# Memory projections in column tiles of 160 over all heads, with the next operand by a masked sum and a VectorE block transpose

## The chip, the cores and the metric

The kernel runs on one NeuronCore of a Trainium2 chip. Its engines work side by side, each on its own list of instructions: PE (TensorE, matmuls; PEld is its weight loading), DVE (VectorE), ACT (ScalarE), POOL (GpSimd) and SP (SyncE, which here only issues transfers). The metric is the device time of one execution in microseconds. A profile is one further execution, with every instruction's start and duration.

## The reference

The program is the forward and the backward pass of a layer: a recurrent memory transformer A, gated by a SwiGLU block B. What the change touches is A, for one batch of S = 2048 tokens of width D = 640, 32 heads of 128, a memory of M = 8 rows and segments of 32 tokens:

```python
mem = mem0
outs = []
for s in range(n_seg):                       # 64 segments
    xs = x[:, s * seg_len:(s + 1) * seg_len, :].copy()
    h = jnp.concatenate([mem, xs], axis=1)   # 8 + 32 rows
    q = jnp.einsum('btd,dhe->bhte', h, Wq)
    k = jnp.einsum('btd,dhe->bhte', h, Wk)
    v = jnp.einsum('btd,dhe->bhte', h, Wv)
    scores = jnp.einsum('bhqe,bhke->bhqk', q, k) * scale
    scores = jnp.where(mask[None, None], scores, -1000000000.0)
    p = _softmax(scores, axis=-1)
    o = jnp.einsum('bhqk,bhke->bhqe', p, v)
    o = jnp.einsum('bhte,hed->btd', o, Wo)
    mem = o[:, :M, :].copy()
    outs.append(o[:, M:, :])
```

The result is `x + s * g`, with `s` from A and `g` the gate from B; the gradients of all inputs and weights are outputs too. The eight memory rows of a segment come out of the segment before it, so the 64 segments form a chain, forward and, for the gradients, backward.

## The kernel before

Six phases follow each other: layer norm; B forward, which also transposes B's weights; A forward (`phase3_Afwd`); the output rows that are still missing (`phase3b_out`); A backward (`phase4_Abwd`); the weight gradients of A (`phase6_Awgrads`); and B backward with the rest. In `phase3_Afwd` and `phase4_Abwd` the instructions of each engine are kept in the order in which they are written (`in_order`). Each of these phases is a loop over the 64 segments. A step of the loop is `chain(t, gap)`: the work on the memory rows, each part of which needs the one before it, with calls of `gap(...)` between the parts. In the gaps stand pieces of work that are free of the chain: the attention of the ordinary tokens in tiles of three segments. Such a tile has eight units of four heads, spread over three steps as 3, 3 and 2 units. WARM names short matmuls whose results nobody reads.

**A forward step.** `hx` holds the operand: 640 rows of D as 5 chunks of 128 partitions, and 32 columns, 8 of them memory rows of this segment and 24 later tokens that ride along. `packed_half` (L346) multiplies it with Wk, Wq and Wv. Four column tiles of PE work side by side, each on 32 output partitions and 512 columns. The memory attention follows (L539 to L580), and its result stands in `oTm`, 128 partitions by 32 heads by 32 columns. `packed_out` (L362) projects it with Wo. The heads are split in two halves and the 640 columns in two halves of 320, so four column tiles hold 2 x 2 partial results in the PSUM bank `pm`, after 16 rounds of four matmuls. `fold_add` (L375) adds the two halves of the heads: ACT copies 160 columns of the upper 64 partitions (L381), DVE adds them to the lower 64 (L382), twice, with one buffer `fup` used in turn. `fold_turn` (L392) turns the sum of 64 x 320 into the layout of `hx` by six small matmuls with a selection matrix (L398), and DVE copies the 8 memory columns into the next `hx` (L594). The sum itself goes to DRAM as FS (L595). The 24 riding columns are loaded from the transposed tokens XNT four steps at a time (`ride_ld`, L464) and copied into `hx` by POOL (`ride`, L487).

The fillers around this place: gap G4 has the softmax of the third unit (`soft`, L650), whose exponentials run on ACT, and the normalisations (`norm`, L666): a reciprocal on DVE (L671), a multiplication on POOL (L672) and a POOL transfer (L673) for each unit. Gap G5, between `fold_add` and `fold_turn`, has the transposes of the first unit's probabilities (`turn_p`, L680) and of queries (`turn_q`, L629), one WARM matmul and the transposes of one weight block (L295). Gap G6, after `fold_turn`, has `turn_p` of the second unit, `turn_q`, and the transposes of keys (`kprep`, L612) in two steps of three.

**A backward step** runs the same way with `gox` in place of `hx`. It starts with the projection by Wo transposed (L1076), and ends with three calls of `packed_out` with 8 columns each, by Wv, Wk and Wq transposed (L1117, L1138, L1140), which add up in one bank. Then come `fold_add`, gap G5 with units of `dprob` and `gmem` and two WARM matmuls, `fold_turn`, the copy into the next `gox` (L1145), two transfers of the sum to GWO (`fold_store`, L386), and gap G6 with DVE work (`dsoft`) and one WARM matmul. In `gap_of`, `ride_ld` and the loads for later steps stand on SP's queue.

**Around the loops.** The transposed weights are made in the gaps of the forward loop (`wT_A_units`, L286; the copies are L90 and L92). After the forward loop FS is copied into HRO and SR by POOL transfers, one for each backward step (`later`, L960 to L977).

Of the kernel before, what the change touches and what calls it, by code (L numbers as in the profile page):

```python
# [9 lines left out]
BF16 = mybir.dt.bfloat16  # L10
# [30 lines left out]
class K:  # L41
# [55 lines left out]
    def setup_consts(self):  # L97
# [16 lines left out]
        self.sel = sel  # L114
        with tc.tile_pool(name="mkscr", bufs=1) as scr:
            self.build_masks(const, scr)
# [35 lines left out]
    def setup_dram(self):  # L152
# [23 lines left out]
        self.FS = mk("FS", (T, 64, 320))  # L176
# [109 lines left out]
def wT_A_units(k, Wq, Wk_, Wv, Wo):  # L286
# [5 lines left out]
    def unit_qkv(nat, dstT, jc):  # L292
        def turn(pt):
            for dc in range(DC):
                nc.tensor.transpose(pt[:, dc, :], nat[:, dc, jc * P:(jc + 1) * P], k.ident[:])  # L295

        def store(st, pt, eng, q):
            k.copy(st[:], pt[:], eng=eng)
            q.dma_start(dstT[jc * P:(jc + 1) * P, :].rearrange("p (dc q) -> p dc q", q=P), st[:])
        return turn, store  # L300
# [61 lines left out]
def packed_out(k, pm, x, W, first, last):  # L362

    nq = x.shape[2]
    for i in range(16):
        for a in range(2):
            for b in range(2):
                h = 16 * a + i
                p0 = 32 * (2 * a + b)
                k.nc.tensor.matmul(pm[p0:p0 + nq, 0:320], x[:, h, :], W[:, h, 320 * b:320 * b + 320],  # L370
                                   start=(first and i == 0), stop=(last and i == 15),
                                   tile_position=(0, p0), skip_group_check=True)


def fold_add(k, pm, pool):  # L375

    nc = k.nc
    fs = pool.tile([64, 320], BF16, name="fsum", tag="fsum")
    for c in (0, 160):
        up = pool.tile([64, 160], F32, name="fup", tag="fup")  # L380
        nc.scalar.copy(up[:], pm[64:128, c:c + 160])  # L381
        nc.vector.tensor_tensor(fs[:, c:c + 160], pm[0:64, c:c + 160], up[:], ALU.add)  # L382
    return fs


def fold_store(eng, dst, fs):  # L386

    for b in range(2):
        eng.dma_start(dst[:, 320 * b:320 * b + 320], fs[32 * b:32 * b + 8, :])


def fold_turn(k, bank, fs):  # L392

    pt = bview(bank, P, k.DC, 8)
    for (dc, p0, c0, w, b) in ((0, 0, 0, 128, 0), (3, 0, 64, 128, 1), (2, 64, 0, 64, 1), (1, 0, 128, 128, 0),
                               (4, 0, 192, 128, 1), (2, 0, 256, 64, 0)):
        kw = {} if w == 128 else dict(tile_position=(0, p0))
        k.nc.tensor.matmul(pt[p0:p0 + w, dc, :], fs[:, c0:c0 + w], k.sel[0:64, b, :], start=True, stop=True,  # L398
                           skip_group_check=True, **kw)
    return pt  # L400


def phase3_Afwd(k, W4, Wv, Wk_):
# [6 lines left out]
    with tc.tile_pool(name="b0", bufs=1) as io, tc.tile_pool(name="b0s", bufs=3) as stp, \  # L410
# [3 lines left out]
        nc.sync.dma_start(xs[:], k.XNT[:, 0:k.NB0].rearrange("(dc p) t -> p dc t", p=P))  # L414
        wq = k.A_Wq.rearrange("(dc p) h e -> p dc (h e)", p=P)
        wo = k.A_Wo.rearrange("h e d -> e h d")
        fetch = [(Wq[:, dc], wq[:, dc]) for dc in range(DC)] + [(Wo[:, h:h + 8], wo[:, h:h + 8]) for h in range(0, H, 8)]
# [23 lines left out]
    with tc.tile_pool(name="ast", bufs=1) as st, tc.tile_pool(name="achain", bufs=1) as ch, \  # L441
# [11 lines left out]
        for i, tt in enumerate(kTs + hxs + qTs + xPs + PTs + [oTm, vt]):  # L453
# [3 lines left out]
        with nc.allow_non_contiguous_dma(reason="tiny mem0 transpose load"):  # L457
            for dc in range(DC):
                nc.sync.dma_start(hxs[0][:, dc, 0:8], k.mem0[:, dc * P:(dc + 1) * P].rearrange("m p -> p m"))
            nc.sync.dma_start(k.m_rows(k.HRO, 0), k.mem0)  # L460
# [3 lines left out]
        def ride_ld(t):  # L464
            x0 = k.NB0 + 24 * t
            b, sub = t // 4, t % 4
            if sub == 0 and x0 < S:
                w = min(96, S - x0)
                rt = ch.tile([P, DC, 96], BF16, name="ride", tag="ride")
                nc.sync.dma_start(rt[:, :, 0:w], k.XNT[:, x0:x0 + w].rearrange("(dc p) s -> p dc s", p=P))  # L470
                rides[b] = (rt, w)

# [13 lines left out]

        def ride(t):  # L487
            b, sub = t // 4, t % 4
            if k.NB0 + 96 * b >= S:
                return  # L490
            rt, w = rides[b]
            nc.gpsimd.tensor_copy(hxs[t % 2][:, :, 8:8 + w // 4], rt[:, :, sub:w:4])

        def chain(t, gap):
# [47 lines left out]
            sTm = ch.tile([40, 2, P], BF16, name="sTm", tag="fsum")  # L542
            nc.scalar.copy(sTm[:], psT.rearrange("p a q h -> p a (q h)"))
            if t + 1 < T:
                ride(t + 1)
# [23 lines left out]
            PTm = ch.tile([104, 8, 16], BF16, name="PTm", tag="fsum")  # L569
# [20 lines left out]
            fs = fold_add(k, pm, ch)  # L590
            gap("G5")
            pt = fold_turn(k, bC, fs)
            nxt = hxs[(t + 1) % 2]
            nc.vector.tensor_copy(nxt[:, :, 0:8], pt[:])  # L594
            nc.gpsimd.dma_start(k.FS[t], fs[:])  # L595
# [119 lines left out]
        ride(0)  # L715
# [110 lines left out]
def gx_ld(k, xs, x0, eng):  # L826
    w = min(P, k.S - x0)
    eng.dma_start(xs[:, :, 0:w], k.GST[:, x0:x0 + w].rearrange("(dc p) t -> p dc t", p=P))
# [13 lines left out]
def phase3b_out(k, Wo, W0, W4):  # L842
# [6 lines left out]
    src = k.WOT.rearrange("(dc p) j -> p dc j", p=P)  # L849
    fetch = [(WoT[:, dc], src[:, dc]) for dc in range(DC)]  # L850
# [112 lines left out]
    for s in range(3):  # L963
# [3 lines left out]
        for b in range(2):  # L967
# [3 lines left out]
            cols = slice(320 * b, 320 * b + 320)  # L971
            later.append((dst[:, :, cols], k.FS[t0:t0 + 3 * (n - 1):3, 32 * b:32 * b + 8, :]))
            t1 = t0 + 3 * (n - 1)
            later.append((k.HRO[r1:r1 + 8, cols], k.FS[t1, 32 * b:32 * b + 8, :]))
    for b in range(2):
# [1030 lines left out]
```

## Time and profile before

| what | value |
|---|---|
| runs of the kernel | 5575.35, 5579.72, 5584.14 us (median 5579.72) |
| the profiled execution | span 5565.9 us, mean granted PE clock 0.956 |
| busy in the span | PE 4988.2 us (90%), PEld 3177.3, DVE 2372.9, ACT 1836.6, POOL 1567.2 |
| forward loop with its start (533 to 1880 us) | 1347 us, PE busy 1216 |
| backward loop with its start (2175 to 3420 us) | 1245 us, PE busy 1152 |
| `packed_out` forward, L370 | 4032 matmuls of 320 columns, 63 calls |
| `packed_out` backward, L370 | 12288 matmuls of 320 columns, 192 calls |
| PE's matmuls waiting in the turn, L398 | 28.3 us forward, 24.2 us backward |

In the lines of the timeline the first number is the start in us from the span's start and the second the time from the first start to the last end in a run of equal instructions (xN of them). `out<-in` are the tiles, and in brackets stands how long the engine had been idle before it and what ended that. A matmul's duration contains its latency, and matmuls overlap, so N matmuls take less than N durations.

### The profile page before, as it was taken

The numbers are of one execution on the slowest core, as the hardware profiler recorded it, in microseconds if no ns is written. First come the engines' busy times: TensorE is split into PE (matmuls) and PEld (weight loads), VectorE is DVE, ScalarE is ACT, GpSimd is POOL, SyncE is SP. The second block draws the span as 40 slices with busy tenths as digits, with TensorE's granted clock in tenths as the row PEclk, the third lists the DMA queues.
The fourth block names the chain that finished last, engine by engine and source line by source line (L and its number), as shares of the span: only waits on it lengthen the run. The fifth ranks groups of instructions, "written<-read, shape, count | busy, mean of one in ns | idle before, by whom it ended". The sixth has DMA issues, their size and how long they took to land. (4 is left out here: it accounts for less than half of the span.)

```text
span 5565.9 us, 167384 instructions
## 1 busy us (share of the span) xinstructions
PE 4988.2 (90%) x67526; PEld 3177.3 (57%) x67870; DVE 2372.9 (43%) x7485; ACT 1836.6 (33%) x5040; POOL 1567.2 (28%) x2606
## 2 busy tenths in 40 slices
PE   4988989999999786999999997999999999999999
PEld 2544555555555453656666664666566656657565
DVE  5743555555555423444454542233233323311451
ACT  2432465555555522333333331232123222301111
POOL 0000244444444313333333333243223322310000
PEclk9999999999999787999999998999999999999999
DMA  7563456556555465666666665343334333546332
GB/s 252 185 206 95 139 170 174 168 167 175 162 164 154 125 202 170 182 189 187 184 185 186 181 171 126 89 121 97 83 93 121 93 85 95 141 161 214 104 119 92
DMA packets 1007174, 835.88 MB, mean 150 GB/s; under 512 B 505131, under 2 KB 894919, under 8 KB 1003083
## 3 DMA queue, kind: packets, MB, share of 16 engines
q1 hardware_dynamic: 760275, 570.63, 36.2%
q0 software_dynamic: 92560, 149.71, 9.5%
q10 hardware_dynamic: 153564, 104.81, 6.5%
q8 instruction: 535, 8.77, 0.7%
q14 instruction: 240, 1.97, 0.1%
HBM read 511.81 MB, written 324.39 MB: 150 GB/s over the span
## 5 line engine op out<-in xcount | busy, mean ns | idle before, releaser
L1460 PE MATMUL wg<-gr,hr 120*128 120x512 bf16 (+1 forms) x2640 | 591.0, 385 | 16.9 <-DVE dST L1392 12.9
L1438 PE MATMUL g<-w,gT 128*128 128x320 bf16 x3840 | 548.9, 300 | 0.0
L1460 PEld LDWEIGHTS <-hr 120*128 120x128 bf16 (+1 forms) x2640 | 258.6, 99 | 341.3 <-issue 49.0
L1438 PEld LDWEIGHTS <-gT 128*128 128x128 bf16 x3840 | 368.9, 98 | 136.6
L251 POOL DMA_DIRECT2D r<-GOS x256 | 143.0, 563 | 798.3 <-PE r6p L1402 749.3
L90 DVE CAST wgo<-wg 128x512 bf16<-128x512 f32 x72 | 47.5, 688 | 586.1 <-issue 280.1
L351 PEld LDWEIGHTS <-hx 128*32 128x32 bf16 x7680 | 178.3, 96 | 167.9 <-issue 8.4
L90 DVE CAST stg<-bank 128x512 bf16<-128x512 f32 x256 | 177.1, 692 | 206.7 <-PE bank L351 194.1
L370 PEld LDWEIGHTS <-gkv 128*8 128x8 bf16 x8192 | 190.9, 88 | 104.3 <-DVE gkv L1069 24.6
L661 ACT ACTIVATE xP<-xsp,xnm 120x120 bf16<-120x120 f32 (+1 forms) x704 | 239.9, 374 | 8.6 <-DVE xnm L657 5.4
L92 ACT CAST wgo<-wg 128x512 bf16<-128x512 f32 x48 | 25.8, 589 | 638.2 <-PE wg L1460 638.2
L1447 DVE TENSOR_TENSOR ghacc<-ghacc,g 128x320 f32<-128x320 f32 x240 | 117.2, 488 | 277.9 <-PE g L1438 277.9
L1405 ACT CAST gr<-r6p 120x512 bf16<-120x512 f32 (+1 forms) x176 | 103.1, 586 | 362.3 <-PE r6p L1402 340.0
L1220 POOL DMA_DIRECT2D DSR<-gdS x176 | 101.7, 578 | 424.4 <-DVE gdS L1218 391.1
L710 POOL DMA_DIRECT2D OR<-xv x163 | 93.8, 576 | 425.2 <-ACT xv L709 295.5
L92 ACT COPY gT<-t6g 128x960 bf16<-128x960 bf16 (+5 forms) x216 | 166.8, 792 | 120.0 <-PE t6g L1421 119.5
L672 POOL TENSOR_TENSOR xP<-xP,xrz 120x480 bf16<-120x480 bf16 x163 | 161.7, 992 | 149.7 <-DVE xrz L671 99.7
L1218 DVE SCALAR_TENSOR_TENSOR gdS<-gdp,Dx,gPr 120x120 bf16<-120x120 f32 (+1 forms) x680 | 182.9, 331 | 0.0
L1421 PE MATMUL t6g<-ident,gr 120*128 120x120 bf16 (+1 forms) x2112 | 171.1, 220 | 3.6 <-DVE wgo L90 3.1
L370 PE MATMUL bank<-Wo,oTm 128*32 128x320 bf16 x4032 | 173.9, 333 | 0.0
L1289 PE MATMUL gbank<-WqT,ident 128*128 128x512 bf16 x453 | 156.4, 394 | 19.5 <-issue 11.7
L536 DVE COPY vt<-stg 8x512 bf16<-8x512 bf16 x512 | 163.0, 318 | 24.3 <-ACT stg L92 17.2
(360 smaller groups left out, 11183.6 us busy)
## 6 DMA issues: line engine op xcount, KB each, us to landing
QVS<-stg SPq DMA_DIRECT2D x128, 256.0 KB
gqv<-QVS SPq DMA_DIRECT2D x108, 192.0 KB
vTt<-VTD SPq DMA_DIRECT2D x64, 320.0 KB
VTD<-gvT POOLq DMA_DIRECT2D x168, 120.0 KB, 3.4
OR<-xv POOLq DMA_DIRECT2D x163, 120.0 KB, 2.7
DSR<-gdS POOLq DMA_DIRECT2D x168, 112.5 KB, 3.5
dS<-DSR SPq DMA_DIRECT2D x168, 112.5 KB
P<-PR SPq DMA_DIRECT2D x168, 112.5 KB
```

What stands on the lines that cost most here:

```text
L90: return nc.vector.tensor_copy(out, in_)
L92: return nc.scalar.copy(out, in_)
L351: k.nc.tensor.matmul(bank[32 * g:32 * g + 32, :], x[:, dc, :], W[:, dc, c0:c0 + 512], start=(dc == 0), stop=(dc == k.DC - 1), tile_positio ...
L370: k.nc.tensor.matmul(pm[p0:p0 + nq, 0:320], x[:, h, :], W[:, h, 320 * b:320 * b + 320], start=(first and i == 0), stop=(last and i == 15), ...
L536: nc.vector.tensor_copy(vt[p0:p0 + 8, c0:c0 + 512], sv[32 * g:32 * g + 8, b * 512:(b + 1) * 512])
L661: nc.scalar.activation(Pb[0:n, j, 0:n], sp[0:n, j, :], ACT.Exp, bias=nmx[0:n, j:j + 1], scale=k.scale, accum_out=Z[0:n, j:j + 1])
L672: eng.tensor_tensor(Pb[0:n, :, 0:n], Pb[0:n, :, 0:n], bc_last(rz[0:n], n), ALU.mult)
L1218: nc.vector.scalar_tensor_tensor(dS[0:n, j, :], dp[0:n, j, :], Dx[0:n, j:j + 1], Pr[0:n, j, :], op0=ALU.subtract, op1=ALU.mult)
L1289: nc.tensor.matmul((bA if g in ("W1", "G1", "G2") else bB)[:], k.ident[:], WqT[:, 0, 0:512], start=True, stop=True)
L1421: nc.tensor.transpose(pt[:, i - i0, j, :], st["g", u, i][0:n, j * P:(j + 1) * P], k.ident[0:n, 0:n])
L1438: nc.tensor.matmul(pg[:], ring[:, i, j, r0:r0 + P], Ws[qd][i][:, j, 320 * h:320 * h + 320], start=(i == 0 and j == 0), stop=(i == 2 and j ...
L1460: nc.tensor.matmul(accs[dc][:], hr[0:n, tl, dc * P:(dc + 1) * P], st["g", NTL * qd + tl, i][0:n, :], start=(tl == 0), stop=(tl == NTL - 1))
```

## The change

`packed_out` no longer splits the heads. All 32 heads are added up in PSUM, and the four column tiles hold four quarters of 160 columns: 32 rounds of four matmuls of 160 columns where there were 16 rounds of four of 320. `fold_add`, `fold_turn` and `fold_store` go. In their place `next_hx` does two DVE operations: one sum of `pm`, masked to the 8 memory rows of each quarter, and `xr`, the riding rows, into a bf16 tile of 128 x 160, and a transpose of that tile by blocks of 32 x 32 straight into the next `hx` (or `gox`). Both stand directly behind the last projection, ahead of gap G5.

```diff
+        self.memrow = const.tile([P, 1], F32, name="memrow")
+        nc.vector.tensor_reduce(self.memrow[:], sel[:].rearrange("p a b -> p (a b)"), axis=AX.X, op=ALU.add)
...
 def packed_out(k, pm, x, W, first, last):
     nq = x.shape[2]
-    for i in range(16):
-        for a in range(2):
-            for b in range(2):
-                h = 16 * a + i
-                p0 = 32 * (2 * a + b)
-                k.nc.tensor.matmul(pm[p0:p0 + nq, 0:320], x[:, h, :], W[:, h, 320 * b:320 * b + 320],
-                                   start=(first and i == 0), stop=(last and i == 15),
-                                   tile_position=(0, p0), skip_group_check=True)
+    for h in range(k.H):
+        for g in range(4):
+            k.nc.tensor.matmul(pm[32 * g:32 * g + nq, 0:160], x[:, h, :], W[:, h, 160 * g:160 * g + 160],
+                               start=(first and h == 0), stop=(last and h == k.H - 1),
+                               tile_position=(0, 32 * g), skip_group_check=True)
...
+def ride_rows(eng, xr, src, n):
+    src = src.rearrange("(i s) (g c) -> g i s c", s=4, g=4)
+    for g in range(4):
+        eng.dma_start(xr[32 * g + 8:32 * g + 8 + n], src[g])
...
+def next_hx(k, hx, pm, xr, pool, fs=None):
     nc = k.nc
+    if fs is None:
+        fs = pool.tile([P, 160], BF16, name="fsum", tag="fup")
+        nc.vector.scalar_tensor_tensor(fs[:], pm[:, 0:160], k.memrow[:], xr, op0=ALU.mult, op1=ALU.add)
+    nc.vector.transpose(hx[:].rearrange("p c q -> p (c q)"), fs[:])
     return fs
```

In the forward step:

```diff
             packed_out(k, pm, oTm, Wo, True, True)
-            fs = fold_add(k, pm, ch)
+            next_hx(k, hxs[(t + 1) % 2], pm, xr[:, (t + 1) % 4, :], ch)
+            fo = ch.tile([P, 160], BF16, name="fout", tag="sTm")
+            nc.scalar.copy(fo[:], pm[:, 0:160])
+            nc.gpsimd.dma_start(k.FS[t], fo[:])
             gap("G5")
-            pt = fold_turn(k, bC, fs)
-            nxt = hxs[(t + 1) % 2]
-            nc.vector.tensor_copy(nxt[:, :, 0:8], pt[:])
-            nc.gpsimd.dma_start(k.FS[t], fs[:])
             gap("G6")
```

And in the backward step:

```diff
             packed_out(k, pm, gqT, WqT, False, True)
-            fs = fold_add(k, pm, ch)
+            if t > 0:
+                fs = next_hx(k, goxs[(t - 1) % 2], pm, gride(t - 1), ch)
+                nc.gpsimd.dma_start(k.GF[t - 1], fs[:])
...
             gap("G5")
-            if t > 0:
-                pt = fold_turn(k, bC, fs)
-                nc.vector.tensor_copy(goxs[(t - 1) % 2][:, :, 0:8], pt[:])
-            fold_store(nc.gpsimd, k.m_rows(k.GWO, t - 1) if t > 0 else out2f, fs)
             gap("G6")
```

What follows from the new layout:

- The riding rows come from the untransposed XN and GS, in four transfers on SP (`ride_rows`) into `xr`, which holds four steps; the POOL copies (`ride`) go.
- The block transpose leaves row 160 g + 32 c + i of D on partition 32 g + i in chunk c. So Wq, Wk, Wv, the transposed Wo, the tokens of the first block and `gx_ld` are loaded in that order, in four transfers of 32 partitions each.
- The copies of transposed Wq, Wk and Wv write runs of 32 columns, which brings those weights back into D's own order in DRAM.
- FS and the new GF are 128 x 160 per step. Forward, ACT copies the projection for FS. `later` has 30 copies in place of 16, and GWO gets its memory rows from GF by twelve POOL copies in the second of the eight rounds of the weight gradients.
- The first operand of each loop is put together in a tile `f0` (riding rows by a DVE copy, and forward the rows of `mem0` by four transfers on SP) and turned by the same transpose.

## The prediction

> **What bounds the kernel now.** I read the 40-slice strip of the page first (PE at 9 tenths almost throughout), then the busy times by stretch, then the timelines of a forward and of a backward memory step, then the waits of PE. The two loops over the 64 segments are the stretches that the change touches:
>
> ```profile
> 533.00:1880.00 1347.00, 1216.03 (x22770) 744.22 (x22897) 761.38 (x2235) 742.09 (x2463) 551.66 (x785) 0.97 0.56 161
> 2175.00:3420.00 1245.00, 1152.24 (x24663) 757.99 (x24842) 590.37 (x2782) 381.40 (x1233) 422.90 (x771) 0.98 0.64 174
> ```
>
> The columns are the length, the busy us of PE, PEld, DVE, ACT and POOL, the granted clock, the DMA share and GB/s. A forward step lasts 1347/64 = 21.0 us, a backward step 1245/64 = 19.5 us. PE is the only engine near its limit, and all engines run in written order, so a step becomes shorter only by what leaves PE's own line: its matmuls, and its waits. The end of a forward step:
>
> ```profile
> 1017.87 2.36 PE L370 MATMUL bank<-Wo,oTm 128*32 128x320 bf16 x64
> 1018.80 0.98 POOL L672 TENSOR_TENSOR xP<-xP,xrz 120x480 bf16<-120x480 bf16 x1 [2.60 <-DVE xrz L671]
> 1020.16 0.39 PE L680 MATMUL xpp<-ident,xP 120*128 120x120 bf16 x4
> 1020.62 0.29 ACT L381 COPY fup<-bank 64x160 f32<-64x160 f32 x1
> 1020.94 0.32 DVE L382 TENSOR_TENSOR fsum<-bank,fup 64x160 bf16<-64x160 f32 x1
> 1020.96 1.00 POOL L672 TENSOR_TENSOR xP<-xP,xrz 120x480 bf16<-120x480 bf16 x1
> 1021.61 0.32 DVE L382 TENSOR_TENSOR fsum<-bank,fup 64x160 bf16<-64x160 f32 x1 [0.35 <-ACT fup L381]
> 1021.98 0.55 PE L398 MATMUL bank<-sel,fsum 64*128 64x8 bf16 x5 [0.49 <-DVE fsum L382]
> 1022.46 0.39 PE L680 MATMUL xpp<-ident,xP 120*128 120x120 bf16 x4
> 1023.16 1.05 PE L351 MATMUL bank<-Wk,hx 128*32 128x512 bf16 x16
> ```
>
> After the projection (L370) ACT and DVE alternate for two half sums (L381, L382). PE waits for them inside the turn (L398); then come the G6 fillers and the next step's first projection. The last lines to compare are of a backward step:
>
> ```profile
> 2703.16 2.35 PE L370 MATMUL gbank<-WqT,gqT 128*8 128x320 bf16 x64
> 2706.92 0.55 PE L398 MATMUL gbank<-sel,fsum 64*128 64x8 bf16 x5 [0.50 <-DVE fsum L382]
> 2707.51 0.20 DVE L1145 CAST gox<-gbank 128x40 bf16<-128x40 f32 x1 [0.64 <-PE gbank L398]
> 2707.86 2.34 PE L351 MATMUL gbank<-WoT,gox 128*32 128x512 bf16 x40
> ```
>
> **What is removed, and what waits next.** Times here count from the start of the projection.
>
> Forward. PE has finished the G5 fillers at about 3.2. Now it spends until 4.47 on the turn and its waits. Without it the G6 transposes of xP (L680) are next, and these need the second POOL multiplication (L672). In the lines above this multiplication starts at 3.09; the shortest usual distance from a multiplication to its transposes in the loop is 1.30 us (1191.73 to 1193.03, 1254.28 to 1255.58). So PE would stop there until 4.39: a wait on POOL takes the place of the one on DVE. From these transposes to the next step's first projection it is 0.69 us in steps with three units (5.28 - 4.59) and 0.52 in steps with two. By place in the group of three: t%3=1: 3.09 + 1.30 + 0.69 = 5.08 against 5.28, gain 0.20. t%3=0: multiplication at 3.15, 5.14 against 5.22, gain 0.08. t%3=2: multiplication at 2.48, 2.48 + 1.30 + 0.52 = 4.30 against 4.82, gain 0.52. Twenty of each: 20 x 0.80 = 16 us. The first three steps have no such units and win about 1.3 us each, 4 us. Forward: -20 us, far under the 74 that the removed lines suggest.
>
> Backward. There is no such unit behind the turn, only one warming matmul of 512 columns. After the last projection PE's G5 work ends at about 3.1 us (two-unit steps; the first turn matmul stands at 2706.25, 3.09 after the start at 2703.16) or 3.3 (three-unit); the warming matmul adds 0.22. The next Wo projection starts now 4.7 after the start (2707.86 - 2703.16). It would start at 3.3 or 3.5, if the operand is there. Gains 1.37 once and 1.17 twice in three steps, mean 1.24.
>
> **The operand chain that replaces it.** One masked sum on DVE: L382 moves 160 columns from PSUM in 0.32 us; L1218, which also takes a per-partition scalar, needs 0.33 us for 120, so about 0.37 for 160. The VectorE block transpose of 128x160 bf16 is not in the trace. From below it is bounded by the vt copy (L536, 512 columns of bf16 in 0.318 us, so about 0.2), from above by a slow pass of a whole 512 (L1736, 0.686). I take 0.32, the row with 160 columns. The page "VectorE: DVE Perf Modes" of the Trainium skill, section "The three transpose paths", gives 311 ns for 128x128; an estimate from it is 0.34 us, and no run here shows it. With some 0.25 us from the last matmul's start to the read and 0.06 for each handover the operand is there about 1.06 us after the last matmul starts. Backward that start is at 2.1, so 3.2 to 3.3: just under PE's fillers; with 0.69 for the transpose it would cost 0.2 to 0.4 us per step, 15 us. Forward the sum also stands behind the third reciprocal on DVE (done at 3.0), so the operand comes at 3.8, covered by the POOL wait to 5.08. Behind the waiting sum on DVE stand the copies of the turned xP (0.40) and, backward, the gdS pass; both come earlier than now.
>
> **The projection itself.** 64 pairs of weight load and matmul with 320 columns become 128 with 160. Four column tiles run together. From the lines above, 16 rounds of 320: (2.36 - 0.30)/15 = 137 ns a round; 10 rounds of 512 (L351): (2.34 - 0.38)/9 = 218 ns. The slope is 0.42 ns per column and 3 ns are fixed, so 160 columns take about 70 ns: 32 x 70 = 2.24 us against 16 x 137 = 2.19, +0.05. That needs 256 PE instructions in 2.24 us. The two nearest rows:
>
> ```profile
> 1011.39 0.96 PE L541 MATMUL bank<-qmT,kT 128*40 128x8 bf16 x32
> 1016.40 0.59 PE L577 MATMUL bank<-PTm,vt 40*128 40x8 bf16 x32 [0.35 <-ACT PTm L571]
> ```
>
> Without tiles: (0.96 - 0.17)/31 = 25.5 ns a pair; with two row tiles 13.5 ns. At 25.5 ns the call takes 3.26 us, +1.07. The tiled row is nearer and 17.5 ns a pair is slower than it, so I take the column bound, plus 0.04 for instruction supply: the page counts 535 instruction packets, 8.77 MB, so 256 instructions each, in 0.7% of 16 engines, 1.2 us a packet, and a call would use one in 2.24 us. That is +0.09 per call, bounds +0.05 and +1.07. Three calls backward: +0.27. Forward the POOL wait takes it in.
>
> Two rules speak against this. "TensorE: Matmul & The Clock Gate", section "Wait — 56ns, not 53.3ns?", says that starts are never under 25 ns apart; the row tiles above are, and by the rule a call would be 3.2 us. "Runtime: NRT & Kernel Launch", section "Instruction fetch mechanics", has some 20 cycles per instruction; an estimate from it is 4.3 us a call and a time near 5950. L577 ran its 64 instructions at 6.8 ns each, but so short a burst may have been queued, so the trace doesn't refute it.
>
> **The rest, near nothing.** The ride copies leave POOL (0.30 and 0.39 us, L492 and L1024), where they ended no wait of weight. One ride transfer on SP becomes four, some 1 us of issue every fourth step, behind it row loads due a step later. The output copy on ACT takes the place of the first L381 (0.29), and the second goes. FS and GF leave by POOL as one transfer (0.57) where GWO took two (1.05). Fourteen more copies from DRAM to DRAM (0.6 to 1.0 us of POOL each) stand ahead of the bdP product, which is needed 5 us later; without that cover, 14 us in all. Twelve stand in the weight gradients, where POOL is a third busy. The weight turns write runs of 32 columns: 0.49 us on DVE (L90) if the mode holds, about 0.83 if not, and then up to 0.34 x 63 = 21 us, since PE waits for that copy now (23.4 us in all). The prologue puts a transfer, a DVE copy and four small transfers on SP ahead of the k rows: +2 us.
>
> **Sum.** Forward -20, backward 63 x (0.27 - 1.24) = -61, prologue +2: -79 us. The profiled span is 5565.9; it becomes 5487. The median of the runs shown, 5579.7, lies 13.8 above the span, so 5501. The likeliest case's own range is 5470 to 5535.
>
> **The rivals.**
> - Slower: the pairs keep the untiled pace of 25.5 ns. Backward 63 x (3 x 1.07 - 1.24) = +124; forward the POOL wait still hides most and -7 stay, prologue +2: 5699. It decides from +0.5 us a call (63 x (3 x 0.5 - 1.24) = 16, against some 16 left forward), 21 ns a pair. For it: no stretch of 256 instructions in the trace is faster than 4.0 us. Against: the fixed 3 ns per round.
> - Middle: supply costs 0.35 a call, or the next step's rows come late. Backward 63 x (1.05 - 1.24) = -12, forward -20, prologue +2: 5550. For it: DMA is 64% busy; against: DMA waits of PE backward are under 20 us.
> - Better: the POOL multiplications come earlier, and forward gains the full 1.18 in each of 63 steps, 74: 5447. Against: they hang on the exponentials, which don't move.
>
> **How the numbers follow.** Forecast 0.54, slower 0.23, middle 0.15, better 0.08. About 0.2% (11 us) is what a measurement can tell from no change; a third of the middle case lies within it: faster 0.72, same 0.05, slower 0.23. The range 5450 to 5650 holds forecast and middle, and reaches toward the slower case.
>
> **What would show it.** Right: 128 matmuls in 2.3 to 2.4 us; L680 in G6 waiting for POOL forward; backward steps near 18.5 us, forward near 20.7. Wrong: calls of 3 us or more, or PE waiting for the transpose at L351.

## The result and the profile after

The changed kernel takes 5751.14 us (four runs, 5746.38 to 5760.39) against 5578.11 (four runs, 5575.35 to 5584.14) on the same chip: a ratio of 1.0313, 95% interval 1.0291 to 1.0335. It is 173 us slower; the forecast was 77 us faster, and the time lies outside the range. The two profiled executions stand a little further apart, 5758.7 and 5565.9 us.

First the stretches of the two loops in the changed kernel (columns as in the prediction):

```profile
567.00:1903.00 1336.00, 1195.70 (x26422) 779.15 (x26549) 757.33 (x2171) 714.42 (x2400) 535.03 (x725) 0.95 0.56 162
2222.00:3585.00 1363.00, 1146.51 (x35860) 875.41 (x36040) 578.74 (x2700) 341.40 (x1100) 384.28 (x656) 0.95 0.59 160
```

Backward, PE is busy for 1147 us, as long as before, but the loop has become longer around it. Measured from the memory scores of the first step to those of the last, the forward loop went from 1322.8 to 1312.4 us (-10), and the backward loop from 1225.6 to 1369.9 (+144). The rest, some +58, came in outside the loops: the first forward step starts 34 us later than before, and between the two loops 24 more are lost. Behind the backward loop nothing changes.

Now what ended PE's idle time in that backward stretch, and the projections of one backward step and the first of the next on PE's timeline (lines between them left out):

```profile
PE gbank L371 <- issue: 136.1, 95, 3.1
PE gvpt L1172 <- DMA gqv<-QVS: 5.9, 2, 4.1
```

```profile
2799.53 0.99 PE L1111 MATMUL gbank<-dSTm,krow 40*128 40x8 bf16 x32
2800.45 1.20 PE L371 MATMUL gbank<-WkT,gkv 128*8 128x160 bf16 x57
2802.45 1.42 PE L371 MATMUL gbank<-WkT,gkv 128*8 128x160 bf16 x71 [0.80 <-issue]
...
2804.09 1.06 PE L371 MATMUL gbank<-WqT,gqT 128*8 128x160 bf16 x49
2807.84 1.55 PE L371 MATMUL gbank<-WqT,gqT 128*8 128x160 bf16 x79 [2.69 <-issue]
...
2817.71 2.39 PE L371 MATMUL gbank<-WvT,gkv 128*8 128x160 bf16 x128
```

L371 is the matmul of `packed_out`. The last line is a call as it was predicted: 128 pairs (a weight load and a matmul each) in 2.39 us with the last one's latency, 17.0 ns from start to start. The two calls above it stop in the middle, between two pairs that wait for nothing but each other, and the profile calls this wait "issue": no semaphore and no engine ended it. Three figures of the profiles point at the reason. TensorE's instructions arrive over a DMA queue of their own (q8): 535 packets with 8.77 MB before, 657 with 10.76 MB now, so 16 KB each. Before, 535 packets carried 135,396 matmuls and weight loads, 253 a packet, which leaves room for a few others; I take it as 256, and a call of 128 pairs is then one packet. The smallest spacing of two such packets in the backward loop is 3.38 us before and 3.33 us now. And the pauses fall where one packet has run out and PE goes on only after the next has landed: the packet that landed at 2801.44 is followed by the matmuls from 2802.45, the next one, landed at 2806.20, by those from 2807.84.

From the first to the last matmul's start, the three backward calls last on average 2.38 (WvT), 3.09 (WkT) and 4.12 us (WqT); before it was 2.14, 2.07 and 2.05. That is 3.33 us a step, 213 in the loop. Some 160 of the 213 us are pauses of over 0.25 us between pairs. Some 39 are pairs that ran at half the granted clock, mostly behind such pauses. The rest is the pace: a call without a pause lasts 2.15 us, before it was 2.05. The forward call went from 2.45 to 3.02, but there the pauses over 0.25 us are few (14 us in the loop, 30 before), and its pairs ran at half clock for 85 us (21 before).

The rest of the change did what was foreseen. The operand chain on DVE:

```profile
L395 DVE SCALAR_TENSOR_TENSOR fsum<-gbank,memrow,gxr x63: 382/384/386, 2240.2 to 3589.7; 128x160 bf16<-128x160 f32 x63
L396 DVE STREAM_TRANSPOSE gox<-fsum x64: 345/345/348, 2218.2 to 3590.1; 128x160 bf16<-128x160 bf16 x64
```

These are the shortest, median and longest of one instruction in ns. Behind the first step of each loop the transpose holds up only weight loads, 11 us in 24 steps; forward, the turn's wait for DVE (28.3 us) is gone, and behind POOL's multiplication there is now one of 10.3 us (L662 is the transpose that stood at L680):

```profile
PE bank L371 <- issue: 11.5, 9, 2.0
PE xpp L662 <- POOL xP L654: 10.3, 15, 0.8
```

### The profile page after: what moved, and what is told of

Its sections match the earlier page's. It is cut to its first block, busy times and chain, and to the rows that moved or that the text cites. A ratio compares the mean times of both kernels' runs of the same rounds, so it can differ in the third digit from the quotient of the medians.

```text
span 5758.7 us, 198271 instructions
## 1 busy us (share of the span) xinstructions
PE 4985.5 (87%) x83090; PEld 3346.4 (58%) x83434; DVE 2364.6 (41%) x7364; ACT 1770.9 (31%) x4849; POOL 1531.3 (27%) x2466
## 3 DMA queue, kind: packets, MB, share of 16 engines
q8 instruction: 657, 10.76, 0.8%
## 5 line engine op out<-in xcount | busy, mean ns | idle before, releaser
L371 PEld LDWEIGHTS <-gkv 128*8 128x8 bf16 x16384 | 291.0, 88 | 93.7 <-issue 60.7
L371 PE MATMUL gbank<-WqT,gqT 128*8 128x160 bf16 x8192 | 192.0, 253 | 87.5 <-issue 87.3
L371 PEld LDWEIGHTS <-gqT 128*8 128x8 bf16 x8192 | 165.0, 94 | 101.2 <-issue 99.4
L1220 ACT ACTIVATE gks<-gkp 128x96 f32<-128x96 f32 (+1 forms) x352 | 71.4, 264 | 484.2 <-PE gkp L1217 468.1
L395 DVE SCALAR_TENSOR_TENSOR fsum<-gbank,memrow,gxr 128x160 bf16<-128x160 f32 x63 | 24.2, 384 | 457.7 <-PE gbank L371 457.7
L371 PE MATMUL gbank<-WkT,gkv 128*8 128x160 bf16 x8192 | 168.4, 237 | 44.6 <-issue 44.5
L371 PEld LDWEIGHTS <-oTm 128*32 128x32 bf16 x8064 | 178.7, 113 | 46.5 <-issue 42.7
L371 PE MATMUL bank<-Wo,oTm 128*32 128x160 bf16 x8064 | 193.7, 267 | 11.5 <-issue 11.5
```

The costliest lines, as they stand in the source:

```text
L371: k.nc.tensor.matmul(pm[32 * g:32 * g + nq, 0:160], x[:, h, :], W[:, h, 160 * g:160 * g + 160], start=(first and h == 0), stop=(last and h ...
```

## The experiments

Theories: **supply** (instructions reach PE too slowly for 128 pairs in a row), **narrow pairs** (a pair of 160 columns costs 25 ns), **chain** (the masked sum, transpose and new layout cost the time). Ratios are to the kernel before, run on the same chip, with their 95% intervals; loop times are from the first to the last step's scores, and a call's length from its first to its last matmul's start, both from the profiled run.

### Half the instructions

```diff
+    for h in range(0, k.H, 2):
+        for g in range(4):
+            c0 = min(160 * g, 320)
+            k.nc.tensor.matmul(pm[32 * g:32 * g + nq, 0:320], x[:, h, :], W[:, h, c0:c0 + 320],
...
-            packed_out(k, pm, gkT, WkT, False, False)
+            packed_wide(k, pm, gkT, WkT, False, False)
```

> The changed kernel, but the three backward projections issue 64 pairs of 320 columns in place of 128 of 160, in the same four column tiles (it leaves out the odd heads and sums other columns; operand chain, loads and all else as in the changed kernel). Column time is the same, the instructions of a call are 128 in place of 256. Supply theory (instructions reach PE in packets of 256 at 3.3 us or more each, so calls of 256 instructions starve): the mean calls of 2.38, 3.09 and 4.12 us fall to about 2.1 each, the backward loop loses 64 x 3.3 = 213 us, time about 5540 (5520 to 5570). Chain theory (the masked sum, the block transpose and the new layout cost the time): within 20 us of 5751. Narrow-pair theory (a pair of 160 columns costs 25 ns wherever it stands) expects the gain too, but the full calls of the changed kernel at 17.3 ns a pair speak against it.

Measured: 5653.59 us, ratio 1.0109 (1.0092 to 1.0126). The calls are back at 2.24, 2.05 and 2.12 us, as the supply theory asks, and the chain theory's 5751 is out. But the loop fell only by 122 us, to 1248.0, where 213 were expected. What stands there in place of the pauses:

```profile
2230.00:3475.00 1245.00, 1143.19 (x24129) 724.16 (x24125) 577.80 (x2701) 344.48 (x1100) 384.73 (x656) 0.93 0.65 174
```

```profile
PE gvpt L1183 <- DMA gqv<-QVS: 45.4, 14, 5.8
PE gvpt L1183 <- DMA gqv<-QVX: 24.1, 7, 5.9
...
PE gbank L382 <- issue: 2.3, 2, 1.9
```

The pauses of the calls (L382) are gone. One step in ten now takes 17.14 us or less, where it was 18.53 before the change, but the slow steps became slower (one in ten above 24.0, against 21.2). PE waits 70 us for the row loads of the fillers (15 before), and the granted clock of the stretch is 0.93 (0.98 before). The records of the clock show it halved for 164 us in 20 stretches; before it was 51 us in seven. All twenty begin at a wait: ten within 1.6 us after the end of a pause of 1.6 to 4.0 us or in its last 0.3 us, ten, the nine longest among them, while a pause of 3.7 to 5.9 us is still running. A second limit lay close under the first, and part of it may belong to the change: the riding rows now come in four transfers, which hold SP's list for 3.3 to 3.7 us every fourth step where one transfer took 0.39, and the row loads stand behind them. Of the 70 us of waits, 42 come 15 to 22 us after the start of such a group, in 7 us out of the 78 of four steps; before, with one transfer, 4 of 15 do. No run tests this by itself.

### The old kernel with split pairs

The edit is made in a copy of `packed_out`, which the three backward calls use.

```diff
     for i in range(16):
+        for c in (0, 160):
             for a in range(2):
                 for b in range(2):
...
+                    k.nc.tensor.matmul(pm[p0:p0 + nq, c:c + 160], x[:, h, :], W[:, h, 320 * b + c:320 * b + c + 160],
...
```

> The kernel before, with one edit: each backward pair of 320 columns is split into two of 160 in the same column tile, so 128 pairs a call. Layout, fold, turn and loads are the old ones. Supply theory: the calls take the lengths of the changed kernel (sum of the three about 9.6 us against 6.26), time 5578 + 63 x 3.3 = about 5785 (5740 to 5800), with the pauses at one place of the 256-instruction packet and 17.3 ns a pair between pauses. Narrow-pair theory: the same total, but an even 25 ns a pair and no pauses. Chain theory: 5578 + 17 = 5595.

Measured: 5790.71 us, ratio 1.0360 (1.0336 to 1.0385). Calls of 2.21, 3.16 and 4.15 us, backward loop 1438.8, +213 on the kernel before.

```profile
PE gbank L384 <- issue: 150.9, 102, 3.4
```

```profile
2809.17 0.86 PE L384 MATMUL gbank<-WqT,gqT 128*8 128x160 bf16 x38
2812.17 2.79 PE L384 MATMUL gbank<-WqT,gqT 128*8 128x160 bf16 x90 [2.14 <-issue]
...
2824.58 2.39 PE L384 MATMUL gbank<-WvT,gkv 128*8 128x160 bf16 x128
```

One edit, twice the pairs, brings the whole loss of the calls into a kernel that has the old layout, the old fold and the old loads. And it isn't the narrow pair: calls without a pause take 2.39 us here too, and the others lose most of their time in one piece. The 90 pairs in 2.79 us above took 29 ns each because they ran at half clock behind their pause (2812.69 to 2816.10 in the records of the clock).

### Work added inside the calls

```diff
+        if between and h % 8 == 4:
+            between()
...
+            def plain():
+                nc.tensor.matmul(bB[:], k.ident[:], WqT[:, 0, 0:512], start=True, stop=True)
+            packed_out(k, pm, gkT, WkT, False, False, plain)
...
+            packed_out(k, pm, gqT, WqT, False, True, plain)
```

> The changed kernel, with four plain 512-column matmuls added inside each of the gkT and gqT projections (after every 32 pairs), 8 x 0.218 = 1.74 us of PE work more in each backward step, and only 16 instructions. Supply theory: the added work runs while PE would have waited for instructions, so the pauses (7 + 54 + 101 us in single gaps over 0.25 us, 213 us with the short ones) shrink and the time stays within -20 to +40 us of 5751. All theories in which PE itself is busy or waits at the end of the step: 63 x 1.74 = +110 us, about 5861.

Measured: 5819.40 us, ratio 1.0408 (1.0392 to 1.0425); the loop 1410.4, +40 on the changed kernel.

```profile
PE gbank L373 <- issue: 35.3, 50, 2.4
```

The total is outside the range that I gave to the supply theory, but my price for the added work was wrong: a call without a pause went from 2.15 to 3.86 us, so a plain matmul between tiled ones costs 0.43 us, not 0.22, and the added work is 8 x 0.43 x 64 = 219 us a loop. Of these only 40 show. PE's pauses in the stretch of the loop fell by 138 us, 101 of them waits for issue in the calls, and the time at half clock fell from 126 us to 40, which is worth some 43. So about half of the added work fits into time in which PE was waiting for instructions in the calls, and a fifth is paid for by the clock, which fell less often.

### Only the forward half of the change

The backward loop, its loads and the weight gradients are those of before; forward all is new.

```diff
-            packed_out(k, pm, gqT, WqT, False, True)
-            if t > 0:
-                fs = next_hx(k, goxs[(t - 1) % 2], pm, gride(t - 1), ch)
+            packed_pair(k, pm, gqT, WqT, False, True)
+            fs = fold_add(k, pm, ch)
```

> The forward loop and its loads as in the changed kernel, the backward loop, its loads and the weight gradients as before. By the landmarks of the two traces: +34 us up to the first forward step (loads in four pieces of 32 partitions), -11 in the forward loop, nothing behind it: about 5600 (5590 to 5615). If the supply theory is right the remaining 150 us of the 173 are all on the backward side; if the loads in pieces were the main cost, most of the loss would stay: 5650 or more.

Measured: 5605.75 us, ratio 1.0035 (1.0015 to 1.0055). The first forward step starts 35 us late, the forward loop takes 1314.4 us (-8). So nearly all of the loss is on the backward side, as the supply theory asks, and the forward half alone doesn't pay for its loads.

### The permuted loads over all partitions

```diff
-    src = src.rearrange("(g c i) n -> g i c n", g=4, i=32)
-    for g in range(4):
-        eng.dma_start(dst[32 * g:32 * g + 32], src[g])
+    src = src.rearrange("(g c i) n -> c g i n", g=4, i=32)
+    for c in range(5):
+        eng.dma_start(dst[:, c], src[c])
```

> The changed kernel, with each permuted load (Wv, Wk, xs, Wq, WoT and the small ones for gX) made of five transfers over all 128 partitions, one per 32-column chunk, in place of four transfers over 32 partitions each. Same bytes, same layout in SBUF. Piece theory (a transfer that writes only 32 partitions is slow, and this made the +34 us up to the first forward step and the +15 in the output projection): these two fall to about +5 together, time about 5751 - 40 = 5711 on the scale of the first measurement. Rival (number and order of transfers in the queue, or the chip's clock): unchanged within 10 us, since there are now more transfers, not fewer.

Measured: 5873.02 us, ratio 1.0511 (1.0491 to 1.0530): much worse, and both sides of the expectation missed. The lines show the weights' queue from 60 to 200 us (packets, MB, share of the 16 DMA engines' time), in the kernel before, in the changed one and in this one:

```profile
q0 software_dynamic: 1456, 13.11, 22.9%
```

```profile
q0 software_dynamic: 1552, 13.11, 37.3%
```

```profile
q0 software_dynamic: 5424, 13.12, 49.7%
```

The same 13.1 MB hold the DMA engines 1.6 times as long in the changed kernel, and 2.2 times here, in 3.5 times as many packets. So the loads in the new row order are dear, and a transfer over all 128 partitions is no cure. Which part of the order does it isn't settled.

### Bursts that nothing waits for

```diff
+                for (n, w) in ((1536, 160), (1024, 320)):
+                    pb = psE.tile([P, 320], F32, name=f"burst{w}", tag=f"acc{w // 320}")
+                    for i in range(n):
+                        g = i % 4
+                        nc.tensor.matmul(pb[32 * g:32 * g + 8, 0:w], k.ident[:, 0:8], xn_all[:, i // 4 % NT, 320 - w:320],
+                                         start=(i < 4), stop=(i > n - 5), tile_position=(0, 32 * g), skip_group_check=True)
```

The burst of 512 pairs in the middle of the backward loop is made the same way and not shown.

> The kernel before with bursts of pairs of the changed kernel's form (8 weight columns, four column tiles) that nothing waits for: 512 pairs of 160 columns in the middle of the backward loop, and behind all other work of TensorE, while the DMA engines are almost idle, 1536 pairs of 160 columns and then 1024 pairs of 320. Supply theory, with a packet of 256 instructions every 3.3 us or more as a limit of its own: the first quiet burst (3072 instructions, 12 packets) takes about 40 us with pauses once in 128 pairs and 17.3 ns a pair between them; the second (2048 instructions at 17 ns each) takes 35 us without pauses; the one in the loop 13 us. If packets are late only because the DMA engines are 64% busy in the loop: 26.6, 35 and 13. If nothing limits the supply: 26.6, 35 and 8.9.

PE's timeline at the end of the kernel, where from 5612 to 5654 us the instruction packets are all that the DMA engines move (11 packets, 0.18 MB, 4 GB/s):

```profile
5608.29 2.93 PE L1931 MATMUL burst<-xn_all,ident 128*8 128x160 bf16 x157
5611.64 2.39 PE L1931 MATMUL burst<-xn_all,ident 128*8 128x160 bf16 x128 [0.42 <-issue]
5615.39 2.39 PE L1931 MATMUL burst<-xn_all,ident 128*8 128x160 bf16 x128 [1.36 <-issue]
5619.41 2.39 PE L1931 MATMUL burst<-xn_all,ident 128*8 128x160 bf16 x128 [1.63 <-issue]
...
5654.21 33.99 PE L1931 MATMUL burst<-xn_all,ident 128*8 128x320 bf16 x995 [0.83 <-issue]
```

This is the supply by itself: 128 pairs, a pause, 128 pairs, a pause, to the end of the 160-column pairs. The 1536 pairs take 43.8 us, more than my 40; a packet every 3.48 to 4.18 us. Such a cycle has three parts: the next packet starts 1.1 to 1.7 us after PE has gone on, its own transfer takes 0.9 to 1.3 us, and PE goes on 1.2 to 1.6 us after it has landed. The quiet burst first stopped after 157 pairs, so PE had no more than 314 instructions in hand at its start. At 320 columns (34 ns a pair) 995 pairs run without a pause. The 512 pairs in the middle of the loop took 13.2 us, with 13 expected. So the limit is there without any other traffic. (The run as a whole: 5685.23 us, ratio 1.0174, 1.0146 to 1.0202.)

### The second limit: fewer loads, and none

Two loads of the backward loop were taken out in turn, in the changed kernel and in the one with half the instructions. First the turned values vT are loaded once and used in all steps:

```diff
-            vT = ch.tile([P, H, 40], BF16, name="vTt", tag="vTt", bufs=1)
-            nc.sync.dma_start(vT[:], k.VTD[tl][:, s])
+            if t == T - 1:
+                vts.append(ch.tile([P, H, 40], BF16, name="vTt", tag="vTt", bufs=1))
+                nc.sync.dma_start(vts[0][:], k.VTD[tl][:, s])
+            vT = vts[0]
```

> The run with half the instructions (64 pairs of 320, odd heads left out), and the turned values vT (320 KB, 20 of the 215 MB of the backward loop) are loaded for the first step only and used in all (their other 63 loads are left out, so dP is that of the first step's values). In that run the steps that nothing disturbed fell from 18.5 to 17.2 us, but the loop came out 22 us longer than before: PE waited 70 us for row loads (15 before) and lost some 55 us more at half clock, mostly behind such waits. Transfer theory (the loop cannot be shorter than its bytes at 174 to 176 GB/s, and the pauses hurt the clock): without 9% of the bytes the waits for rows fall under 30 us, the clock comes back, and the loop falls by 80 to 120 us: about 5650 - 100 = 5550. Rival (a power limit on the clock, which grows with the share of work): the waits may fall, but the clock stays near 0.93 and the time falls by less than 50.

Measured: 5613.26 us, ratio 1.0066 (1.0046 to 1.0086), loop 1222.0 (-26). The loop moves 161 GB/s, so no rate of 175 binds it, and PE still waits 69 us for rows, 13.5 of them at once. The theory of the bytes falls. The signs that the rival named, a clock near 0.93 (0.94 here) and less than 50 us, did come; the run with kept rows below decides on it.

> The changed kernel with the same 63 loads of vT left out. Supply theory: packets of instructions do not come faster, the pauses in the three projections (sum of the mean calls 9.6 us) stay within 10%, and the time stays within 25 us of the changed kernel (5751 on the first chip, some 5765 here). Contention theory (packets are late because the loop's transfers hold the engines): fewer bytes shorten the calls, and the time falls by 50 us or more.

Measured: 5733.42 us, ratio 1.0282 (1.0244 to 1.0320), calls of 2.29, 2.90 and 4.01 us: together 4% shorter, and a loop of 1342.8 us (-27). The calls, and the time by the ratios (17 us less than the changed kernel), lie within what the supply theory allowed.

Then the rows of the fillers are kept instead (vT is loaded again):

```diff
             g = i % 6 if early else (i - len(pro) + 1) % NG
+            if g in kept:
+                uu["l", tl, qd] = kept[g]
+                return
```

> The run with half the instructions (odd heads left out), and the row loads of the backward fillers (q, v, gO and P, four buffers in a ring) are made for the first four units of the loop only; the units after them use the rows that lie there (their loads are left out, so their gradients are not those of their own rows). Leaving out vT's loads had shortened the loop by only 26 us, at 161 GB/s, with PE still waiting 69 us for these rows: they are issued when a buffer of the ring comes free and need some 12 us. Late-row theory: without these loads PE's waits for rows and nearly all half-clock stretches that follow them go, and the loop falls from 1248 us to some 64 x 17.4 = 1115 (1090 to 1150), the time to about 5510. Rival (a power limit that halves the clock for 10 us at a time without a wait before it, and takes back what is gained): the loop stays above 1180.

Measured: 5500.33 us, ratio 0.9862 (0.9834 to 0.9890), and a loop of 1113.5 us, with 1115 expected.

```profile
2226.00:3320.00 1094.00, 1051.65 (x23664) 693.87 (x23840) 571.43 (x2685) 338.83 (x1095) 384.26 (x654) 1.00 0.52 133
```

The granted clock is 1.00. The loop is 134 us shorter than with its loads. The 70 us of waits and half of the 150 us at half clock that went (164 then, 14 now) make 145, a little more, since part of the time at half clock lay in the waits themselves. With the waits the half clock went, at a higher pace of the work, so there is no sign of a power limit. The undisturbed steps now show what the change saves: 17.8, 17.8 and 17.1 us by their place in the group of three, where the kernel before has 18.9, 18.9 and 18.5, a mean gain of 1.20 us.

Why the rows come late can be read from one case in the trace of the run without vT's loads, first on SP, then on PE:

```profile
2608.73 3.72 SPq L398 DMA_DIRECT2D gxr<-GS  x4
2613.57 2.28 SPq L1175 DMA_DIRECT2D gqv<-QVS  x4
```

```profile
2628.33 0.56 PE L1187 MATMUL gvpt<-ident,gqv 120*128 120x120 bf16 x4 [4.96 <-DMA gqv<-QVS]
```

The ring has four buffers, and a unit's loads are issued when the unit four places ahead of it has left its buffer. Here they stood behind the four transfers of the riding rows, and PE waited 4.96 us for the rows issued from 2613.57 us on. More buffers, or the riding rows on another queue, were not tried.

> The changed kernel with the same row loads left out, which takes about half of the bytes out of the loop. Supply theory (a packet of 256 instructions takes 3.5 to 4 us also when the DMA engines are idle, as in the quiet burst): the three projections still take more than 9 us a step together (9.6 now, 6.3 before) and the loop stays above 1320 us (1370 now). Contention theory: their sum falls under 7.5 us and the loop under 1250.

Measured: 5699.35 us, ratio 1.0216 (1.0192 to 1.0240). Loop 1312.1, calls of 2.19, 2.71 and 4.01 us, 8.91 together: a little under both bounds that I gave, but far from the other theory's. With the bytes moved in the stretch down to 113 GB/s from 160, four fifths of the 3.33 us a step are still there. The pauses over 0.25 us in the calls fell only from 160 to 144 us; the rest of the fifth is the clock, since the pairs ran at half clock for 24 us where it was 77. So without the loop's row loads the pauses are a tenth shorter, and nine tenths are the supply's own.

### A version that beats both

The changed kernel's aim, a shorter way from the last projection to the next operand, can be had without more instructions: keep the 64 pairs of 320, and let the turning matmuls add the two halves of the heads.

```diff
+    cs = pool.tile([P, 320], BF16, name="fcast", tag=tag, bufs=bufs)
+    k.nc.vector.tensor_copy(cs[:, 0:160], pm[:, 0:160])
+    k.nc.scalar.copy(cs[:, 160:320], pm[:, 160:320])
...
-        k.nc.tensor.matmul(pt[p0:p0 + w, dc, :], fs[:, c0:c0 + w], k.sel[0:64, b, :], start=True, stop=True,
+        k.nc.tensor.matmul(pt[p0:p0 + w, dc, :], cs[:, c0:c0 + w], k.sel2[:, b, :], start=True, stop=True,
```

> The kernel before, with 64 pairs of 320 columns kept, but the sum of the two head halves moved into the turning matmuls: one copy of PSUM to bf16, half on VectorE and half on ScalarE at the same time, then the six turning matmuls contract all 128 partitions with a matrix that has ones for both halves; the folded rows that go to DRAM are added behind, off the path. No instruction more on TensorE, no permuted load. The wait of the turn for the second sum (22.7 us backward, 0.5 a step) goes, and the fold's last 0.6 us leave the path: backward at most 63 x 0.75 = -47, forward -16 as in my prediction (the wait on POOL remains). If the backward loop is held by its row loads (174 to 176 GB/s in both traces) and the clock, half of the 47 comes back: ratio to the kernel before between 0.988 and 0.994.

Measured: 5565.30 us, ratio 0.9961 (0.9941 to 0.9981): faster, by 22 us, and less than the 0.988 to 0.994 expected. In the profiles the gain is forward (loop 1299.8, -23). Backward one step in ten takes 17.95 us or less, against 18.53, but the loop is 1231.3, +6:

```profile
PE gvpt L1197 <- DMA gqv<-QVS: 18.2, 12, 3.4
PE gvpt L1197 <- DMA gqv<-QVX: 12.7, 6, 3.6
```

The 23 us at the turn are gone, and 31 us of waits for rows (15 before) and 88 us at half clock (51 before) stand in their place.

## Why the prediction was wrong

- **The column bound of a call** (+0.05 us): right in kind. A call without a pause takes 2.15 us from the first to the last start, against 2.05, so +0.11 where +0.09 stood with the supply term; 17.0 ns a pair. The pace of 25.5 ns, on which the slower rival rested, is not what happened.
- **Instruction supply** (+0.04 us a call): the step that failed. I had the right quantity, one packet of 256 instructions a call, but took the packet's own transfer, 1.2 us, for its cycle and concluded that it fits into 2.24 us. The cycle is 3.3 us at best in the loop and 3.5 to 4.2 in the quiet burst. The trace of before showed both the spacing of 3.38 us and, as the rival's text says, no stretch of 256 instructions under 4.0 us. Measured in its place: +0.24, +1.02 and +2.07 us a call backward, where +0.27 a step stood in the sum and 3.33 came. These figures hold the half clock behind the pauses too, some 39 of the 213 us. The calls grow along the step, probably because the product with the k rows (64 instructions) and two of the calls follow each other with hardly anything slow between them. Calls of 3 us or more were the sign of being wrong that I had named. The bound of +1.07 a call, taken from the nearest slow row, was almost exactly the mean (+1.11), but by luck: its mechanism, an even 25.5 ns a pair, was another.
- **The operand chain** (gain 1.24 us a backward step): right. 0.384 and 0.345 us against 0.37 and 0.32, and little waits for it. In the run with kept rows the steps are 1.20 us shorter than undisturbed ones before, against 1.24. And loop +144 less calls +213 leaves -69, against 63 x 1.24 = 78.
- **Cover for late loads**: I put the late rows into the middle rival with 0.15, since PE waited under 20 us for them. That wait was small while the steps were long. With the calls short again, the loop is 22 us longer than before instead of 69 shorter, and the run with kept rows (-112) shows that rows and clock take the difference. So even with a free supply the forecast of -61 backward would not have come. One term of the prediction under "near nothing" may be part of it: the ride's four transfers on SP were put at some 1 us of issue, with the rows behind them due a step later, and they take 3.3 to 3.7. How much of the 70 us of waits that makes, no run separates.
- **Forward** (-20): the loop won 10. The POOL wait appeared, but with 10.3 us where 54 (74 - 20) were to be hidden in it. In its place the call grew by 0.56 us on average, 35 in the loop, and most of that was the clock: the loop ran at half clock for 116 us, where it was 68. The prediction had no term for the clock.
- **Prologues and loads** (+2): mis-sized; +58 came. I counted transfers and issues and not how long the permuted rows hold the DMA engines: the weights' queue 37.3% against 22.9% of them. PE waits 15.5 us for the first tokens and 17.1 us for the first rows of the output projection, which stood at 3.9 and 0.6 before. That is 28 of the 58; where the rest arose was not followed up.

Against the two rules that I weighed: "TensorE: Matmul & The Clock Gate", section "Wait — 56ns, not 53.3ns?" (never under 25 ns between starts), doesn't hold for matmuls in four column tiles, which start every 17.0 ns here. "Runtime: NRT & Kernel Launch", section "Instruction fetch mechanics", gave an estimate of 4.3 us a call; the calls that a full queue feeds take 2.15, but the sustained supply of the quiet burst, 3.5 to 4.2 us per 256 instructions, is close to it. The closeness is in the number alone: the section speaks of an issue rate per instruction, and here pairs went out at full pace, 8.5 ns an instruction, until a packet had run out. I wrote that a burst of 64 instructions doesn't refute the estimate, and still gave it no place among the rivals.

## What to carry to other kernels

Count TensorE's instructions as well as its columns: a change that halves the width of matmuls doubles the stream, and a stretch of some hundred instructions at under 13 ns each runs dry, while the share of busy time still says that PE is the bound. Look for the smallest spacing of the instruction packets, not for how long one takes. And before pricing a gain on a loop's main engine, ask which loads are just in time: a wait of 15 us in 1225 was the visible part of a limit that took back some 90. Look, too, at what a change adds to the queue on which those loads stand.

## What the runs showed of the hardware

- PE's instructions come in packets of 256 with hardly more than one packet in hand (the quiet burst first stopped after 314 instructions), and when PE waits for them, packets start 3.5 to 4.2 us apart even when nothing else moves. "Advanced Engine Details and Errata", section "ISA Cache", says that a line holds 256 instructions and that there are only two lines; the pauses after exactly 128 pairs agree with the 256, and the 314 instructions with the two lines. "Runtime: NRT & Kernel Launch", section "Instruction fetch mechanics", calls the cost of a boundary mostly hidden; at 17.0 ns a pair it is mostly 1.1 to 1.6 us of idle time in some 3.8.
- The granted clock can halve after short pauses. In the changed kernel's backward loop it is at half for 126 us in 32 stretches of mostly 3.4 us, most of them at or right behind a pause of 1 to 3 us. The pauses need not be in one piece: in the forward loops of both kernels PE had been idle for 1.05 to 2.0 us of the 3.4 us before each of the 48 falls, mostly in two or three waits under 1 us. In these loops 24 more windows of 3.4 us had 1.0 us or more of idle time and brought no fall. "TensorE: Matmul & The Clock Gate", section "Part 1: The HAM clock gate (the "warmup" mystery)", names an idle window of about 3.4 us for this; here pauses shorter than that were enough.
- A full matmul of 512 columns between matmuls in column tiles cost 0.43 us, twice its 0.21 beside its like (two in 0.59 us, one in 0.38).
- The same 13.1 MB of weights held the DMA engines 1.6 and 2.2 times as long when their rows were loaded in the new order, in four transfers of 32 partitions and in five of 128.
